# A gated mix of two attention layers on one core: key-value products in column tiles, numerators in three fixed tiles

## The chip, the core and the metric

The kernel runs on one core of one Trainium2 chip. A core has a matrix engine (TensorE: PE for its matmuls, PEld for its weight loads), a vector engine (DVE), an activation engine (ACT), a general engine (POOL) and a queue engine (SP) that issues most of the transfers. Matmuls write to PSUM, eight banks of 512 fp32 columns on 128 partitions; DVE and ACT read it from there. The metric is the device time of the whole program in microseconds, the median of several runs. Three runs of the kernel before took 323.28, 323.5 and 323.81 us.

## What is computed

Two attention layers work on the same 2048 x 640 input, 32 heads of 20, and a gate mixes them. Layer A is linear attention: two softmaxes (of a projection and of its negative) over 20 features of each head are the key and query features. Layer B is causal softmax attention in four segments of 512, with a memory between the segments.

```python
# layer A, per head
pq, pk = q @ w_phi, k @ w_phi
phi_q = concat(softmax(pq), softmax(-pq))
phi_k = concat(softmax(pk), softmax(-pk))
kv = phi_k.T @ v                      # features x 20
z = phi_k.sum(over tokens)            # features
o = (phi_q @ kv) / (phi_q @ z + 1e-6)
a = o @ wo
# layer B: per segment, softmax(q k^T) v mixed with (phi(q) @ M) / (phi(q) @ z);
# M and z grow by phi(k)^T v and phi(k) after each segment
out = g * a + (1 - g) * b             # g = sigmoid(x . gate_w)
```

Activations and weights are bf16, sums fp32. The kernel multiplies the layer-A query and key weights with `w_phi` first, so that features come from one product.

## The kernel before

The order of the instructions on each engine is written out by hand: within `tc.manual_schedule` every engine executes in the order in which the code emits. The part that the change edits runs in four stages.

- **Keys and values** (`emit_a1`, `emit_zmove`, lines 229 to 257). For each of 16 chunks of 128 tokens PE makes the key features' logits and the values, ACT takes exponentials of both signs into `Ek` and copies the values into `vA`, DVE sums each head's 20 features (L243) and takes reciprocals (L246), POOL multiplies to `EkSn` (L247). Two transfers per chunk move `EkSn` into `Z` (L255), so that a column sum over the 32 slices of `Z` becomes an elementwise sum on DVE.
- **Key-value products** (`emit_kv`, `emit_kvn`, from L404). The 640 features are five blocks `j` of 128, with two signs. For each (`j`, sign) PE accumulates over the chunks: weights are 128 columns of `EkSn`, the moving side is `vA`, 140 columns (the seven heads that the block touches), or two pieces of 80 where the block crosses head 16 (`j` = 2). DVE masks the result into `kvn` (L383). Between them DVE adds the `Z` slices, each to slice 0 (`emit_zadd`, L261): 9, then 4, then 18. The five loads of 800 KB with the weights for layer B and the two output projections stand on SP right behind the last `Z` moves (L428, L433).
- **Query features and the first denominators** (L515). `emit_pq` makes ten 128 x 1024 blocks of query logits (two halves of the tokens, five blocks); ACT takes the exponentials into `Eq`. After the fifth, PE transposes the `Z` sum (L266); DVE folds its 32 columns with 31 adds (`emit_zz`, L274) and masks the result into `kvd` (L277). After the ninth, PE makes the denominators of the first four chunks (L453), and `first_chain` turns them into the factors `cs`.
- **Numerators** (L583). For each of 16 chunks and each sign: DVE multiplies the numerator by its factor into `tt` (`emit_tt`, L489), PE makes the next half of a layer-B projection (`emit_next_half`: 36 halves for k, q and v, evicted by ACT, L553), and PE makes the numerator of the next chunk into the tile of this sign (`emit_num`, L443; two tiles, one per sign). In the first two chunks of each batch of four PE also makes denominators of the next batch in a tile of their own. POOL adds the two signs (L604), and SP transposes the sum into `oTA` (L620). One chunk in four, three activations and a POOL add (L625 to L629) make layer B's key features; two exponentials more stand in the last two chunks (L618).

Layer B (L635 on) then runs in steps of two heads' groups: PE makes logits with row tiles of 32 (L681), ACT takes exponentials (L685), POOL masks (L692), PE multiplies with v (L735), and projections and output products (`half_item`, `out_items`) fill the rest by a written plan. The first output products of the plan read `oTA` of the last chunk.

Of the kernel before, what the change touches and what calls it, by code (L numbers as in the profile page):

```python
# [15 lines left out]
def kernel(  # L16
# [15 lines left out]
    nc = tc.nc  # L32
# [196 lines left out]
    def emit_a1(sc):  # L229
# [17 lines left out]
        nc.gpsimd.tensor_tensor(  # L247
# [11 lines left out]
    def emit_zadd(ts):  # L259
        for t in ts:  # L260
            nc.vector.tensor_tensor(out=Z[:, 0, :], in0=Z[:, 0, :], in1=Z[:, t, :], op=ALU.add)  # L261
# [7 lines left out]
    def emit_zz(zt_ps):  # L269
        nc.vector.tensor_copy(out=zt, in_=zt_ps)  # L270
        ztv = zt.rearrange("p j (s a h b) -> p j s h b a", s=2, h=2, b=2)
        nc.vector.tensor_copy(out=zz, in_=ztv[:, :, :, :, 0, 0])
        for w in range(1, 32):
            nc.vector.tensor_tensor(out=zz, in0=zz, in1=ztv[:, :, :, :, w // 16, w % 16], op=ALU.add)  # L274
        nc.vector.tensor_tensor(out=zcol, in0=zz[:, :, :, 0], in1=zz[:, :, :, 1], op=ALU.add)
        for sgn in range(2):
            nc.vector.tensor_tensor(out=kvd[:, sgn, :, :, 0], in0=wmask,  # L277
                                    in1=zcol[:, :, sgn:sgn + 1].to_broadcast([P, KC, H]), op=ALU.mult)
# [79 lines left out]
    def emit_kv(j, sgn, scs):  # L358
        h0, h1 = (P * j) // DH, (P * j + P - 1) // DH + 1
        bk, off = int(j > 2), 0  # L360
        n = (h1 - h0) * DH
        b0 = h0 // 16
        if (sgn, j) not in kv_tiles:
            kv_tiles[sgn, j] = w2tile("kv_ps")
            if j < 2:
                kv_tiles[sgn, j + 3] = kv_tiles[sgn, j]
        for sc in scs:
            if h1 <= 16 or h0 >= 16:
                o = 321 * b0 + (h0 - 16 * b0) * DH
                parts = [(off, vA[:, sc].rearrange("p b n -> p (b n)")[:, o:o + n])]  # L370
            else:
                n0 = (16 - h0) * DH
                parts = [(off, vA[:, sc, 0, h0 * DH:320]),
                         (off + n0, vA[:, sc, 1, 0:n - n0])]
            for o, rhs in parts:
                nc.tensor.matmul(kv_tiles[sgn, j][:, bk, o:o + rhs.shape[-1]],
                                 lhsT=EkSn[:, sc, sgn, j * P:(j + 1) * P], rhs=rhs,
                                 start=(sc == 0 and o == off), stop=(sc == NCH - 1 and o == parts[-1][0]))

    def emit_kvn(j, sgn):  # L380
        h0, h1 = (P * j) // DH, (P * j + P - 1) // DH + 1
        g0 = TH[j][0]
        nc.vector.tensor_tensor(  # L383
            out=kvn[:, sgn, j, h0 - g0:h1 - g0, :],
            in0=kv_tiles[sgn, j][:, int(j > 2), 0:(h1 - h0) * DH].rearrange("p (h d) -> p h d", d=DH),
            in1=wmw[:, j, h0 - g0:h1 - g0, None].to_broadcast([P, h1 - h0, DH]), op=ALU.mult)
# [4 lines left out]
    def emit_pq(qb, j):  # L391
        Eq = Eq0[:, j] if qb == 0 else a3e.tile([P, 2, HB], BF16, name="Eq")
        pq = w2tile("pq")
        for half in range(2):
            for c in range(KC):
                nc.tensor.matmul(pq[:, half, :], lhsT=WqA[:, c, j * P:(j + 1) * P],  # L396
                                 rhs=xq[:, 2 * qb + half, c],
                                 start=(c == 0), stop=(c == KC - 1))
        pqf = pq.rearrange("p b n -> p (b n)")
# [4 lines left out]
    emit_zadd(range(1, 10))  # L404
    PAIRS = [(js, sgn) for js in ((0, 3), (1, 4)) for sgn in range(2)]
    for js, sgn in PAIRS:
        for j in js:
            emit_kv(j, sgn, range(14))
    for js, sgn in PAIRS:
        for j in js:  # L410
            emit_kv(j, sgn, range(14, NCH))
        for j in js:
            emit_kvn(j, sgn)
    emit_zadd(range(10, 14))
    for sgn in range(2):
        emit_kv(2, sgn, range(NCH))
        emit_kvn(2, sgn)
    emit_gate()
    emit_zadd(range(14, 32))
# [7 lines left out]
    for W, src in ((WkB, B_wk), (WqB, B_wq), (WvB, B_wv)):  # L427
        nc.sync.dma_start(out=W, in_=src.rearrange("(c p) n -> p c n", p=P))  # L428
# [5 lines left out]

    BATCH = [list(range(c, c + 4)) for c in range(0, NCH, 4)]
    NB = 4

    def emit_num(ch, sgn):
        qb, qc = divmod(ch, HB // P)
        t = nps.tile([P, 2, 512], F32, name=f"num{sgn}")  # L440
        for n, (j, bk, lo, hi) in enumerate(PIECES):
# [4 lines left out]
                             start=(n in FIRST), stop=(n in LAST))  # L446
        return t[:, :, 0:320].rearrange("p b (h e) -> p b h e", e=DH)

    def emit_den(t, ch, k):
        qb, qc = divmod(ch, HB // P)  # L450
        for sgn in range(2):
            for j in range(KC):
                nc.tensor.matmul(t[:, k, sgn].rearrange("p h e -> p (h e)"),  # L453
# [4 lines left out]
    def den_tile():  # L458
        return dps.tile([P, NB, 2, H, 2], F32, name="den")

    def emit_rr(t, n, o=0):
        rr = a3w.tile([P, NB, 2, H], F32, name="rr")
        nc.vector.reciprocal(out=rr[:, 0:n], in_=t[:, o:o + n, :, :, 1])
        return rr, emit_uu(t, rr, n, o)

    def emit_uu(t, rr, n, o):
        uu = a3w.tile([P, NB, 2, H], F32, name="uu", bufs=1)
        nc.vector.tensor_tensor(out=uu[:, 0:n], in0=t[:, o:o + n, :, :, 0], in1=rr[:, 0:n], op=ALU.mult)
        return uu

    def emit_dsum(uu, n):
# [3 lines left out]
        return dd  # L475

# [17 lines left out]
    def first_chain(dt):  # L494
        rr, uu = emit_rr(dt, NB)
# [19 lines left out]
    for qb in range(2):  # L515
        for j in range(KC):
            emit_pq(qb, j)
            if (qb, j) == (0, KC - 1):
                z_den = w2tile("z_den")
                zt_ps = emit_z(z_den[:, 0])  # L520
            if (qb, j) == (1, 0):
                emit_zz(zt_ps)
                open_stages()
            if (qb, j) == (1, 3):
                dt = z_den[:, 1].rearrange("p (k s h e) -> p k s h e", k=NB, s=2, e=2)
                for n in range(NB):
                    emit_den(dt, n, n)
    emit_gS()
    first_chain(dt)
    aps_stack.close()  # L530
    nps_stack = ExitStack()
    nps, dps, last_pps, pps = [nps_stack.enter_context(tc.tile_pool(
        name=n, bufs=b, space=bass.MemoryType.PSUM, reuse_waits="tile"))
        for n, b in (("nps", 1), ("dps", 1), ("last_pps", 1), ("pps", 2))]
    oTA = resB.tile([P, NCH + 1, KC, P], BF16, name="oTA")
    Msb = resB.tile([P, G, 4, DH + 1], F32, name="Msb")
    Mbd = resB.tile([P, G, 4, DH + 1], BF16, name="Mbd")

    def emit_half_mm(ps, part, sc, half):
        W = {"k": WkB, "q": WqB, "v": WvB}[part]  # L540
        for cc in range(KC):
            nc.tensor.matmul(ps, lhsT=xq[:, sc // 4, cc, sc % 4 * P:(sc % 4 + 1) * P],  # L542
                             rhs=W[:, cc, half * 320:(half + 1) * 320],
                             start=(cc == 0), stop=(cc == KC - 1))

# [18 lines left out]
    for vB in vBs:  # L564
        nc.gpsimd.memset(vB[:, :, :, DH:DH + 1], 1.0)
# [3 lines left out]
              for half in range(2)]  # L569

    def emit_next_half():
        if halves:
            emit_half(last_pps if len(halves) % 3 == 1 else pps, *halves.pop(0),
                      nc.scalar.copy if halves else nc.vector.tensor_copy)
# [5 lines left out]
    nums = [emit_num(0, 0)]  # L580
    emit_next_half()
    nums.append(emit_num(0, 1))
    for ch in range(NCH):  # L583
# [4 lines left out]
        for sgn in range(2):  # L588
            emit_tt(tt, sgn, nums[sgn], cs_of[ch])
            emit_next_half()  # L590
            if (ch, sgn) in ((4, 1), (9, 1), (14, 1)):
                emit_next_half()
            if ahead and k < 2 and sgn == 0:
                if k == 0:
                    dt = den_tile()
# [492 lines left out]
```

## Time and profile before

One execution was profiled. It took 323.34 us, and the span from its first to its last instruction is 321.6 us; the granted clock of TensorE is 1.00 throughout. By stage, in us (PE is a busy time, so pipelined matmuls that overlap count once):

| stage | from | to | PE | DVE | ACT | POOL |
|---|---|---|---|---|---|---|
| weights folded, first tokens | 0.0 | 10.3 | 8.6 | 4.2 | 5.3 | 8.5 |
| keys and values | 10.3 | 56.2 | 45.9 | 35.6 | 36.2 | 36.9 |
| key-value products | 56.2 | 66.7 | 10.5 | 10.2 | 1.8 | 2.8 |
| query features, first denominators | 66.7 | 89.7 | 23.0 | 19.2 | 17.6 | 4.2 |
| numerators | 89.7 | 131.6 | 41.3 | 35.5 | 24.4 | 34.3 |
| layer B and the outputs | 131.6 | 321.6 | 179.8 | 119.4 | 166.8 | 122.4 |

A row of the timeline reads: start, length of the group, engine, line, operation, what it writes and reads, shapes, how many; in brackets the idle time of the engine before it and what ended it. A long group of short instructions is one row. A row "SPq" is the time in which SP issues a transfer; the transfer lands later (2.6 us after its issue for a transpose into `oTA`, by the median).

### The profile page before, as it was taken

Reading aid. Unit: us, or ns where it says so; the run is one execution under the profiler, and the core shown is the slowest. Engines: PE = TensorE matmul, PEld = TensorE weight load, DVE = VectorE, ACT = ScalarE, POOL = GpSimd, SP = SyncE. Lnnn points to the kernel's source line nnn. Section 1 sums busy time; section 2 is a strip of 40 time slices with the busy share of each in tenths; the row PEclk is TensorE's granted clock in tenths of the full one; section 3 lists DMA queues with packets and bytes.
Section 4 is the critical chain, followed back from the end, with each engine's and each line's share of the span. In section 5 each row is a group of like instructions: output and inputs, shape, how many; then the busy total and the mean of one; then the engine's idle time right before and its main releaser. Section 6 shows DMA issues by size and latency. Waiting matters only on the chain.

```text
span 321.6 us, 9481 instructions
## 1 busy us (share of the span) xinstructions
PE 309.1 (96%) x3904; PEld 214.1 (67%) x3904; DVE 224.1 (70%) x447; ACT 252.0 (78%) x322; POOL 209.1 (65%) x308
## 2 busy tenths in 40 slices
PE   8999999999999999999999999999999999999995
PEld 7888877964577788555566566666566666655663
DVE  3477997998799797486768577676865755454463
ACT  4677888248945545999998999999998998998953
POOL 8588599302268789756657667777776676666550
PEclk9999999999999999999999999999999999999999
DMA  7947935691016796886331354462476463322132
GB/s 227 204 117 195 209 101 142 196 366 57 0 35 110 114 149 99 156 100 78 58 67 35 66 92 83 88 94 54 78 117 93 67 125 65 74 75 52 47 88 82
DMA packets 91812, 34.19 MB, mean 106 GB/s; under 512 B 79866, under 2 KB 91770, under 8 KB 91770
## 3 DMA queue, kind: packets, MB, share of 16 engines
q1 hardware_dynamic: 91194, 32.95, 50.3%
q10 hardware_dynamic: 576, 0.66, 0.7%
q8 instruction: 30, 0.49, 0.7%
q14 instruction: 12, 0.10, 0.1%
HBM read 6.42 MB, written 2.62 MB: 28 GB/s over the span
## 4 chain that ended last, share of the span: by engine, by line
PE 36%; ACT 18%; DVE 4%; POOL 3%; issue 3%; DMA 1%; ACTq 0%; DVEq 0%
ACT PT L685 17%; PE st_ps L681 8%; PE proj L813 8%; PE nda L735 6%; PE proj L869 5%; PE proj L542 4%; PE num L443 2%; DVE Eq L845 1%; ACT ek L841 1%; PE nda L748 1%; DVE td L772 1%; PE nda L743 1%; POOL oB L775 1%; DMA oTA<-oA 1%; PE st_ps L991 1%
## 5 line engine op out<-in xcount | busy, mean ns | idle before, releaser
L685 ACT ACTIVATE PT<-st_ps 128x1024 bf16<-128x1024 f32 x160 | 153.6, 1024 | 14.6 <-PE st_ps L681 12.2
L692 POOL TENSOR_SCALAR_AFFINE_SELECT PT<-PT 128x512 bf16<-128x512 bf16 (+1 forms) x130 | 85.9, 679 | 47.6 <-ACT PT L685 47.4
L735 PEld LDWEIGHTS <-PT 128*128 128x128 bf16 x1280 | 40.4, 96 | 8.8 <-issue 5.2
L247 POOL TENSOR_TENSOR EkSn<-Ek,krec 128x1280 bf16<-128x1280 bf16 x16 | 37.5, 2358 | 8.8 <-DVE krec L246 8.1
L735 PE MATMUL nda<-vB,PT 128*128 128x21 bf16 x1240 | 41.4, 173 | 0.3
L869 PEld LDWEIGHTS <-xTf 128*128 128x128 bf16 x300 | 26.5, 97 | 15.8 <-issue 6.7
L875 DVE CAST Z<-proj 128x320 bf16<-128x320 f32 x44 | 20.8, 486 | 22.0 <-PE proj L869 20.9
L235 PEld LDWEIGHTS <-xTf 128*128 128x128 bf16 x240 | 27.1, 113 | 5.8
L243 DVE TENSOR_REDUCE ksum<-Ek 128x64 f32<-128x1280 bf16 x16 | 23.6, 1475 | 7.6 <-ACT Ek L239 7.4
L681 PE MATMUL st_ps<-Z 32*128 32x512 bf16 (+3 forms) x256 | 25.0, 299 | 3.8 <-ACT PT L685 3.6
L489 DVE TENSOR_TENSOR tt<-num,rr 128x640 f32<-128x640 f32 x32 | 24.8, 802 | 4.9 <-POOL rr L482 2.2
L239 ACT ACTIVATE Ek<-pk 128x640 bf16<-128x640 f32 x32 | 20.8, 702 | 9.2 <-PE pk L235 8.2
L604 POOL TENSOR_TENSOR oA<-tt 128x640 bf16<-128x640 f32 x16 | 24.6, 1547 | 4.6 <-DVE tt L489 3.4
L813 PE MATMUL proj<-WkA,oTA 128*128 128x320 bf16 x160 | 27.1, 299 | 0.1
L681 PE MATMUL st_ps<-Eq 32*128 32x512 bf16 (+3 forms) x256 | 25.0, 299 | 2.0 <-ACT PT L685 1.6
L775 POOL TENSOR_TENSOR oB<-td 128x320 bf16<-128x320 f32 x22 | 19.5, 888 | 6.4 <-DVE td L772 4.7
L401 ACT ACTIVATE Eq<-pq 128x1024 bf16<-128x1024 f32 x20 | 19.4, 1021 | 5.4 <-PE pq L396 5.4
L813 PE MATMUL proj<-WvA,oT 128*128 128x320 bf16 x120 | 22.2, 300 | 0.6 <-DVE oTA L822 0.6
L396 PE MATMUL pq<-xTf,WqA 128*128 128x512 bf16 x100 | 22.1, 379 | 0.0
L772 DVE TENSOR_TENSOR td<-nda,rec 128x640 f32<-128x640 f32 x23 | 19.0, 824 | 2.1
L542 PEld LDWEIGHTS <-xTf 128*128 128x128 bf16 x180 | 16.3, 97 | 4.4
L443 PE MATMUL num<-kvn,Eq 128*128 128x240 bf16 (+2 forms) x192 | 18.0, 229 | 0.6 <-DVE tt L489 0.6
(174 smaller groups left out, 551.9 us busy)
## 6 DMA issues: line engine op xcount, KB each, us to landing
Z<-EkSn SPq DMA_DIRECT2D x32, 160.0 KB, 2.7
out_dram<-orow SPq DMA_DIRECT2D x8, 160.0 KB, 1.8
out_dram<-oTA SPq DMA_DIRECT2D x6, 160.0 KB, 1.9
WvA<-in_A_wqkv_dram SPq DMA_DIRECT2D x2, 400.0 KB, 6.7
WkB<-in_B_wk_dram SPq DMA_DIRECT2D x1, 800.0 KB
WqB<-in_B_wq_dram SPq DMA_DIRECT2D x1, 800.0 KB, 6.6
WvB<-in_B_wv_dram SPq DMA_DIRECT2D x1, 800.0 KB, 9.5
WkA<-in_A_wo_dram SPq DMA_DIRECT2D x1, 800.0 KB, 11.2
```

The lines of the kernel that those rows point to most:

```text
L235: nc.tensor.matmul(ps[:, bk, 0:n], lhsT=key_tokens(c, sc), rhs=rhs, start=(c == 0), stop=(c == KC - 1))
L247: nc.gpsimd.tensor_tensor(out=EkSn[:, sc].rearrange("p s (h f) -> p (s h) f", f=DH), in0=Ek.rearrange("p s (h f) -> p (s h) f", f=DH), in1 ...
L443: nc.tensor.matmul(t[:, bk, (lo - 16 * bk) * DH:(hi - 16 * bk) * DH], lhsT=Eqs[qb, j][:, sgn, qc * P:(qc + 1) * P], rhs=kvn[:, sgn, j, lo ...
L489: nc.vector.tensor_tensor(out=tt[:, sgn].rearrange("p (b h) d -> p b h d", b=2), in0=ps, in1=csb, op=ALU.mult)
L542: nc.tensor.matmul(ps, lhsT=xq[:, sc // 4, cc, sc % 4 * P:(sc % 4 + 1) * P], rhs=W[:, cc, half * 320:(half + 1) * 320], start=(cc == 0), s ...
L604: nc.gpsimd.tensor_tensor(out=oA.rearrange("p (h d) -> p h d", d=DH), in0=tt[:, 0], in1=tt[:, 1], op=ALU.add)
L681: nc.tensor.matmul(ps[:, i - i0, o:o + L - c * P], lhsT=kT[32 * i:32 * i + 32, c * P:(c + 1) * P], rhs=qT[32 * i:32 * i + 32, c * P:L], st ...
L685: nc.scalar.activation(out=PT[:, i0:i0 + 2], in_=ps, func=ACT.Exp, scale=SCALE_B)
L692: nc.gpsimd.affine_select(out=v, in_=v, pattern=[[0, n_i], [1, P]], compare_op=ALU.is_ge, fill=0.0, base=0, channel_multiplier=-1)
L735: nc.tensor.matmul(nd[:, j, i], lhsT=block(st, c)[:, i, (j - c) * P:(j - c + 1) * P], rhs=vB[:, c, 4 * st.g + i, :], start=(c == 0), stop= ...
L813: nc.tensor.matmul(ps, lhsT=oT[:, k % KC], rhs=W[:, k % KC, hs], start=(k == 0), stop=(k == n - 1))
L869: nc.tensor.matmul(ps, lhsT=xq[:, sc // 4, k, sc % 4 * P:(sc % 4 + 1) * P], rhs=W[:, k, half * 320:(half + 1) * 320], start=(k == 0), stop ...
```

## The change

Four things are edited.

1. The key-value products, but for the first chunk, are made in two column tiles: weights of 64 columns of `EkSn`, the moving side the four heads (80 columns) that these 64 features touch, written to partitions 0 to 63 or 64 to 127 of one PSUM tile that holds both signs. Blocks 0 to 3 run over chunks 1 to 13 first, then over 14 and 15; block 4 comes last. One `kvn` instruction covers both signs.
2. The `Z` adds are made in two halves of 320 columns, and `emit_zz` in slices of three and two blocks, without its first copy; `kvd` is one instruction. The last chunk's `EkSn` is made by DVE. The gate's `emit_gS` moves ahead of the last adds.
3. The layer-B and output weights wait for `kvn` of block 3 by a POOL copy into `WvB`, which is loaded first. The v projections of chunks 0 and 4 move ahead of the numerators.
4. Numerators go round three fixed tiles, made three steps ahead, and the denominators of the next batch lie in columns 320 to 447 of the numerator tiles of the batch's second chunk. All projection halves use one pool of two tiles. The key-feature activations and the two late exponentials are placed at other steps (`KEYS`, `EXPS`); the last projection half then stands in chunk 14 and the last POOL add in chunk 13, where both stood in chunk 15. Layer B's PSUM pools are laid out anew, with one pool for each logits tile.

```diff
@@ emit_a1
-        nc.gpsimd.tensor_tensor(
+        (nc.vector if sc == NCH - 1 else nc.gpsimd).tensor_tensor(
             out=EkSn[:, sc].rearrange("p s (h f) -> p (s h) f", f=DH),
...
     def emit_zadd(ts):
         for t in ts:
-            nc.vector.tensor_tensor(out=Z[:, 0, :], in0=Z[:, 0, :], in1=Z[:, t, :], op=ALU.add)
+            for lo in (0, D // 2):
+                cols = slice(lo, lo + D // 2)
+                nc.vector.tensor_tensor(out=Z[:, 0, cols], in0=Z[:, 0, cols], in1=Z[:, t, cols], op=ALU.add)
@@ emit_zz
-        nc.vector.tensor_copy(out=zz, in_=ztv[:, :, :, :, 0, 0])
         for w in range(1, 32):
-            nc.vector.tensor_tensor(out=zz, in0=zz, in1=ztv[:, :, :, :, w // 16, w % 16], op=ALU.add)
+            for js in (slice(0, 3), slice(3, KC)):
+                nc.vector.tensor_tensor(out=zz[:, js], in0=ztv[:, js, :, :, 0, 0] if w == 1 else zz[:, js],
+                                        in1=ztv[:, js, :, :, w // 16, w % 16], op=ALU.add)
...
-        for sgn in range(2):
-            nc.vector.tensor_tensor(out=kvd[:, sgn, :, :, 0], in0=wmask,
-                                    in1=zcol[:, :, sgn:sgn + 1].to_broadcast([P, KC, H]), op=ALU.mult)
+        nc.vector.tensor_tensor(out=kvd[:, :, :, :, 0], in0=wmask[:, None].to_broadcast([P, 2, KC, H]),
+                                in1=zcol.rearrange("p c s -> p s c")[:, :, :, None].to_broadcast([P, 2, KC, H]),
+                                op=ALU.mult)
@@ emit_kv
+    def emit_kv(j, sgn, scs, group=None):
+        f0, f1 = (P * j, P * j + P) if group is None else (P * j + 64 * group, P * j + 64 * group + 64)
+        h0, h1 = f0 // DH, (f1 - 1) // DH + 1
+        base = (P * j) // DH
+        if j not in kv_tiles:
+            kv_tiles[j] = w2tile("kv_ps")
+        at = {} if group is None else {"tile_position": (0, 64 * group)}
         for sc in scs:
+            parts = [(max(h0, 16 * b), min(h1, 16 * b + 16), b) for b in range(2) if h0 < 16 * b + 16 and h1 > 16 * b]
+            for n, (lo, hi, b) in enumerate(parts):
+                nc.tensor.matmul(kv_tiles[j][f0 - P * j:f1 - P * j, sgn, (lo - base) * DH:(hi - base) * DH],
+                                 lhsT=EkSn[:, sc, sgn, f0:f1],
+                                 rhs=vA[:, sc, b, (lo - 16 * b) * DH:(hi - 16 * b) * DH],
+                                 start=(sc == 0 and n == 0), stop=(sc == NCH - 1 and n == len(parts) - 1), **at)
+
+    def emit_kv_groups(j, scs):
+        for sc in scs:
+            for sgn in range(2):
+                for group in range(2):
+                    emit_kv(j, sgn, [sc], group)
...
-    emit_zadd(range(1, 10))
...
+    emit_zadd(range(1, 7))
+    for j in range(4):
+        for first in ([0], [1, 2, 3], [], [])[j]:
+            for sgn in range(2):
+                emit_kv(first, sgn, [0])
+        emit_kv_groups(j, range(1, 14))
+    for j in range(4):
+        emit_kv_groups(j, range(14, NCH))
+        emit_kvn(j)
+    emit_zadd(range(7, 9))
     for sgn in range(2):
-        emit_kv(2, sgn, range(NCH))
-        emit_kvn(2, sgn)
+        emit_kv(4, sgn, [0])
+    emit_kv_groups(4, range(1, NCH))
+    emit_kvn(4)
     emit_gate()
-    emit_zadd(range(14, 32))
+    emit_gS()
+    emit_zadd(range(9, 32))
...
-    for W, src in ((WkB, B_wk), (WqB, B_wq), (WvB, B_wv)):
+    nc.gpsimd.tensor_copy(out=WvB[:, 0, 0:2], in_=kvn[:, 0, 3, 0, 0:2])
+    for W, src in ((WvB, B_wv), (WkB, B_wk), (WqB, B_wq)):
         nc.sync.dma_start(out=W, in_=src.rearrange("(c p) n -> p c n", p=P))
@@ emit_num, den_view
-        t = nps.tile([P, 2, 512], F32, name=f"num{sgn}")
+        t = nps[(0, 2, 1)[(2 * ch + sgn) % 3]].tile([P, 2, 512], F32, name="num")
...
+    def den_view(t):
+        return t[:, :, 320:448].rearrange("p n (s h e) -> p n s h e", s=2, e=2)
...
+    pqs, vs = [(qb, j) for qb in range(2) for j in range(KC)], list(EARLY_V)
+    for what in "pppppvzppppdvp":
...
-    nps, dps, last_pps, pps = [nps_stack.enter_context(tc.tile_pool(
+    *nps, pps = [nps_stack.enter_context(tc.tile_pool(
         name=n, bufs=b, space=bass.MemoryType.PSUM, reuse_waits="tile"))
-        for n, b in (("nps", 1), ("dps", 1), ("last_pps", 1), ("pps", 2))]
+        for n, b in (("nps0", 1), ("nps1", 1), ("nps2", 1), ("pps", 2))]
...
+    KEYS, EXPS = {1: 0, 5: 1, 9: 2, 11: 3}, {(13, 0): 'k', (14, 0): 'q'}
...
+    def emit_num_at(i):
+        if i < len(order):
+            ch, sgn = order[i]
+            t = nums[ch, sgn] = emit_num(ch, sgn)
+            if ch % 4 == 1 and ch < NCH - 4:
+                for n in range(2):
+                    emit_den(den_view(t)[:, n], ch + 3 + 2 * sgn + n)
+
+    for what in "nnhhn":
...
         for sgn in range(2):
-            emit_tt(tt, sgn, nums[sgn], cs_of[ch])
-            emit_next_half()
...
+            t = nums.pop((ch, sgn))
+            emit_tt(tt, sgn, num_view(t), cs_of[ch])
...
+            if ahead and (k, sgn) in ((1, 0), (1, 1)):
+                emit_rr(rr_n, uu, den_view(t), 2 * sgn, 2)
...
+            emit_num_at(2 * ch + sgn + 3)
+            if ch - 1 in KEYS and sgn == 0:
+                nc.scalar.activation(out=ek, in_=ek, func=ACT.Exp, scale=-1.0)
...
+        if ch - 2 in KEYS:
+            nc.gpsimd.tensor_tensor(out=phik, in0=phik, in1=ek, op=ALU.add)
```

195 lines of the change are left out of this document (85 added, 110 removed).

## The prediction

> **What bounds the kernel now.** I read the page first (busy shares), then the busy time by stage, then the timeline stage by stage, then the chain of waits over the last 200 us.
>
> ```profile
> PE 309.1 (96%) x3904; PEld 214.1 (67%) x3904; DVE 224.1 (70%) x447; ACT 252.0 (78%) x322; POOL 209.1 (65%) x308
> ```
>
> ```profile
> 56.20:66.70 10.50, 10.50 (x201) 10.40 (x200) 10.16 (x22) 1.78 (x3) 2.81 (x2) 1.00 0.78 238
> 66.70:89.70 23.00, 23.00 (x152) 11.26 (x149) 19.22 (x63) 17.63 (x19) 4.16 (x6) 1.00 0.32 109
> 89.70:131.60 41.90, 41.30 (x493) 33.61 (x492) 35.47 (x51) 24.36 (x51) 34.30 (x36) 1.00 0.67 110
> ```
>
> Columns of the stage rows: stretch, its length, busy time (and instructions) of PE, PEld, DVE, ACT, POOL, granted clock, DMA share, GB/s. In the three stages that the change edits, key-value products (56.2 to 66.7), feature products with the first denominators (to 89.7) and numerators (to 131.6), PE is idle for 0.6 us in all, at granted clock 1.00. So time there can be won by shorter PE work or by those gaps; and whatever else is late becomes a new PE gap.
>
> ```profile
> 56.24 10.44 PE L376 MATMUL kv_ps<-vA,EkSn 128*128 128x140 bf16 x192
> ...
> 66.72 10.95 PE L396 MATMUL pq<-xTf,WqA 128*128 128x512 bf16 x50
> ...
> 67.69 9.43 DVE L261 TENSOR_TENSOR Z<-Z 128x640 bf16<-128x640 bf16 x18
> ...
> 77.50 0.44 PE L266 MATMUL z_den<-ident_b,Z 128*128 128x128 bf16 x5
> ...
> 78.85 6.59 DVE L274 TENSOR_TENSOR zz<-zz,zt 128x20 bf16<-128x20 bf16 x31
> ...
> 85.68 0.58 DVE L277 TENSOR_TENSOR kvd<-wmask,zcol 128x160 bf16<-128x160 f32 x2
> ...
> 86.42 1.33 PE L453 MATMUL z_den<-kvd,Eq 128*128 128x64 bf16 x40
> ```
>
> Beside PE runs a second chain that only just keeps up: DVE's Z sums end at 67.69 + 9.43 = 77.12 and PE transposes them at 77.50; DVE's `kvd` ends at 86.26 and PE uses it at 86.42. Slack: 0.4 and 0.2 us.
>
> ```profile
> 100.07 0.56 PE L443 MATMUL num<-kvn,Eq 128*128 128x240 bf16 x6 [0.30 <-DVE tt L489]
> ...
> 131.31 1.54 POOL L604 TENSOR_TENSOR oA<-tt 128x640 bf16<-128x640 f32 x1 [1.26 <-issue]
> ...
> 132.81 1.34 POOL L629 TENSOR_TENSOR Z<-Z,ek 128x640 bf16<-128x640 bf16 x1
> ...
> 132.92 2.57 SPq L620 DMA_TRANSPOSE oTA<-oA  x2
> ...
> 136.90 0.66 PEld L813 LDWEIGHTS <-oTA 128*128 128x128 bf16 x6 [0.48 <-DMA oTA<-oA]
> ```
>
> The gap at 100.07 comes again at 111.05: a numerator waits until DVE has emptied its tile. Into the last stage leads the last `oA`: ready at 132.85, its transpose second in SP's pair at 132.92, landed at about 136.87, where PE waits for it.
>
> **Key-value products.** Before: 128 matmuls of 140 columns and 64 of 80. In the trace the first start 60.8 ns apart, the second 35.8: 7.78 + 2.29 = 10.07 us (the row has 10.44, with 0.2 of last latency). After: 12 of these stay whole (first chunk; 8 x 60.8 + 4 x 35.8 ns = 0.63 us) and 300 of 64 x 80 come in 150 pairs, one per column half.
>
> No row has column tiles, so the pair is bounded. Low end: both stream at once, 35.8 ns. High end: one after the other, 71.6 ns. Nearest rows: the L681 row tiles go two at a time; with 128 columns two start within 4 ns and the next two 66 ns later (133.26), 13 ns above what 128 columns take, so 33 + 13 = 46 ns for 80. And a load with a short matmul never steps faster than in "219.76 1.00 PE nda L735 x40", 25 ns, so 50 for two. I take 48: 7.2 us. The tile shape changes six times (whole to halves and back, three times); around L681 each such change leaves some 0.09 us (L869 at 135.37 streams 0.14 us, L681 starts at 135.60): 0.55 us. Sum 7.2 + 0.63 + 0.55 = 8.4, a gain of **1.7 us** (ends: 3.5 gain, 1.85 loss; break-even for the stage is (10.07 - 1.18) / 150 = 59 ns).
>
> The Trainium skill ("TensorEngine Tiling (Array Packing)", Restrictions) says that column tiling turns Fast Weight Load off, and "TensorE: Matmul & The Clock Gate" (LDWEIGHTS) gives a plain load columns / 1.2 ns. By these, an estimate: 2 x 53 = 107 ns per pair, 16 us, a loss of 7 us in place of my gain. No run here shows it; the trace's loads are all 128 wide, 97 ns long, and at L735 25 ns apart.
>
> **The Z chain.** It must shorten too, since PE reaches the Z transposes at 77.50 - 1.7 + 1.36 (two projection halves, 2 x 0.68 us by the L542 groups, now stand ahead) = 77.2. (a) The last `EkSn` goes from POOL (2.36 us, to 59.01) to DVE: 1280 elements as in L243, 1.49 us, behind POOL's running one: about 56.65 to 58.2. The first Z add before began at 56.70 but lasted 2.66 us, until POOL was done, where the others last 0.49; so adds effectively began at 58.87 and now at 58.2. (b) Adds wait for the one before: 0.526 us apart, 31 of them 16.3 us. Halves wait for the one before last. Length of a half from 20 elements in 0.178 us (L274) and 640 in 0.492: 0.33; independent neighbours overlap by 0.084 (L383: 0.294 long, 0.210 apart): 0.246 apart, 62 of them 15.2 us. If they did not overlap it would be 22.6. (c) Five `kvn` of 280 at 0.294 + 0.146 - 0.084 = 0.36: 1.8 us, 0.5 less than ten. (d) The gate's three small operations (0.69 us) move ahead of the last adds, to which five hand-overs add 0.1. Sum: 58.2 + 15.2 + 1.8 + 0.7 + 0.1 = 76.0, 1.2 us before PE asks. From there `zz` costs as before (a pair must wait 0.17 + 0.04 us for its forerunner, 31 x 0.21), its first copy goes (0.3) and `kvd` is one instruction (0.1 less): `kvd` is ready 7.9 us after the transposes, PE asks after 40 `pq`, 8.64. Cost nothing; the cover is 0.7 us.
>
> **Weight loads held.** A POOL copy makes `WvB` wait for the fourth `kvn`, about 64.0; behind it on SP wait the other four loads, needed from 89 on, and on POOL two memsets and the stage memsets, idle there 19 us before. `WvB` must be in by 75.8; before, as third of its row it landed 9.5 us after issue, as first it will take no longer: 73.6. Nothing, with 2 us of cover; each us later would be a PE gap.
>
> **Numerators.** PE's work is the same (32 x 0.40, halves at 0.68, denominators 0.29 a chunk), only 4 halves stand earlier. With three tiles the two gaps of 0.30 us go: -0.6. DVE needs per batch of four chunks 8 x 0.745 (tt) + 2 x 0.95 + 2 x 0.29 + 0.29 + 0.94 = 9.7 us, PE 8 x 0.40 + 8 x 0.68 + 4 x 0.29 = 9.8: level, so I count a new wait of 0.1. Projection evictions share ACT with the moved exponentials (0.43 and 0.74 in 1.08 us of PE now and then); two tiles of slack hide it.
>
> **The seam.** The k and q exponentials and the last POOL add leave the end. POOL then runs cs, oA 11, add, oA 12, 13, add, 14, 15 without a pause: 1.1 + 5 x 1.53 + 2 x 1.34 after DVE's last reciprocal, so the last `oA` is no earlier against the denominators than before (46 us after their start, less the halves moved), but SP has no turn left ahead of it and lands it 2.65 us later in place of 4.0. By this side I get 0.55 us, by PE's own end 0.6 - 0.1: the same **0.55 us**.
>
> **Sum.** -1.7 - 0.55 = -2.25 us. The profiled execution took 323.34 us (span 321.6, 1.7 around it): 321.1. The median shown, 323.5, is 0.16 above that execution: **321.2**.
>
> **Rivals.** (1) *The tiles overlap fully*, 36 ns: L681's two starts within 4 ns speak for it. PE gains 3.5 us but then asks for Z at 75.4 and gets it at 76.0, so 2.9 + 0.55 count: 320.1. (2) *The tiles take turns*: L681's overlapping matmuls write two banks (line 681, `ps[:, i - i0]`), the two halves here write one. 71.6 ns: 10.74 + 1.18 = 11.9 us, +1.85 - 0.55: 324.8, slower. It decides from 63 ns per pair on. (3) *The loads set the pace*: each 64-column load takes half of the 97 ns of a 128-column row and the two go in turn, 97 ns a pair: 14.55 + 1.18 = 15.7, +5.7 - 0.55: 328.6. For it: 300 loads for 150 streams of 33 ns, nothing to hide them behind; against: 128-wide loads at 25 ns. The rule of the skill quoted above is its extreme. (4) *DVE becomes the bound*: denominators in a numerator's tile hold it until reciprocal and product are done (1.24 us more), DVE is level with PE, and the Z halves overlap less than L383. The 0.55 goes, and up to 2 us of Z wait arises: 321.8 to 323.8, middle 322.9.
>
> **Chances.** Forecast 0.46, (1) 0.20, (2) 0.12, (3) 0.09, (4) 0.13. About 0.2% (0.65 us) is what a measurement of this kernel can tell from no change. Faster: 0.46 + 0.20 + half of (4) = 0.73; within: 0.06; slower 0.21. The range reaches from full overlap with Z adds quick enough not to hold it (3.5 + 0.55: 319.4) and a further 0.7 at the seam, 318.7, to the turn-taking tiles: 325.0; it leaves out (3) and a little at both ends. The forecast's own range is 320.3 to 322.3.
>
> **What would show it.** The key-value group at 64 x 80: 300 matmuls in about 7.8 us (6 and under: rival 1; 12: 2; 15: 3). Z adds 0.25 us apart, the Z transposes with no PE idle before them. No PE wait for `tt` in the numerators beyond 0.1 us, or a new one on the denominators' tiles (4). The last transpose issued right behind its `oA`. The length of the last stage, 190 us, unchanged: if it moves by more than 0.5 us, the sum is wrong in a place where I put nothing.

## The result, and the profile after

Nine runs of each kernel on one chip: 323.43 us before (322.85 to 323.81), 322.30 us after (321.32 to 322.85); ratio 0.9964, 95% interval 0.995 to 0.9979. The forecast was 321.2. The profiled execution of the changed kernel took 322.69 us (span 321.0) where that of the kernel before took 323.34 (321.6): 0.65 us less, and 2.25 were forecast.

The page after, busy time by engine, and the stage rows (stretch, length, busy time of PE, PEld, DVE, ACT, POOL with instructions, granted clock, DMA share, GB/s):

```profile
PE 305.7 (95%) x4024; PEld 209.8 (65%) x4024; DVE 224.3 (70%) x505; ACT 253.0 (79%) x321; POOL 207.7 (65%) x308
```

```profile
56.50:65.20 8.70, 7.37 (x319) 6.66 (x319) 7.26 (x24) 1.72 (x3) 0.64 (x2) 1.00 0.41 104
65.20:91.70 26.50, 26.07 (x173) 13.13 (x170) 23.57 (x120) 18.91 (x21) 5.60 (x9) 1.00 0.45 155
91.70:129.90 38.20, 38.20 (x475) 31.70 (x474) 33.49 (x50) 23.81 (x47) 32.29 (x33) 1.00 0.74 116
```

PE has 3.4 us less to do, but in the products it is now idle for 1.3 of 8.7 us where it was never idle. The numerators have no gap any more. The timeline of the changed kernel says where PE stood (start, length, engine, line, what; in brackets idle time before it and what ended it):

```profile
56.48 6.72 PE L373 MATMUL kv_ps<-vA,EkSn 128*128 128x140 bf16 x283
...
58.34 2.90 DVE L263 TENSOR_TENSOR Z<-Z 128x320 bf16<-128x320 bf16 x12
61.71 1.56 DVE L387 TENSOR_TENSOR kvn<-kv_ps,wmw 128x280 bf16<-128x280 f32 x4 [0.47 <-PE kv_ps L373]
...
64.36 0.74 PE L373 MATMUL kv_ps<-vA,EkSn 128*64 128x80 bf16 x29 [1.16 <-issue]
...
65.14 0.45 DVE L387 TENSOR_TENSOR kvn<-kv_ps,wmw 128x280 bf16<-128x280 f32 x1 [0.93 <-PE kv_ps L373]
...
65.58 1.23 POOL L544 MEMSET vB<- 128x128 bf16 x2 [2.04 <-PE gt_ps L349]
65.64 1.21 DVE L354 TENSOR_SCALAR eg<-eg 128x16 f32<-128x16 f32 x1
...
77.99 0.58 PE L268 MATMUL z_den<-ident_b,Z 128*128 128x128 bf16 x5 [0.43 <-DVE Z L263]
...
129.82 5.22 SPq L661 DMA_TRANSPOSE oTA<-oA  x4
129.88 0.39 PE L723 MATMUL st_ps<-Z 32*128 32x512 bf16 x2
...
130.46 3.04 POOL L653 TENSOR_TENSOR oA<-tt 128x640 bf16<-128x640 f32 x2
...
136.46 0.99 PE L855 MATMUL proj<-WkA,oTA 128*128 128x320 bf16 x6 [1.02 <-DMA oTA<-oA]
```

Three waits are new, and one is larger. In the middle of block 4 PE stands still and waits for nothing that the profile shows ("issue"): 1.36 us from one start to the next. DVE, at 65.14, has stood 0.93 us for that block's `kvn`; then its small operation on `eg`, 16 numbers a partition, takes 1.21 us while POOL's two memsets run. PE waits 0.43 us for Z. And the first product with `oTA` waits 1.02 us for the last transpose.

Start to start, in the two profiled executions:

| | before | after | difference |
|---|---|---|---|
| span start to first product | 56.24 | 56.48 | +0.24 |
| first product to first `pq` | 10.48 | 8.77 | -1.71 |
| first `pq` to Z transposes, less the two early projection halves (1.36) | 10.78 | 11.38 | +0.60 |
| Z transposes to first numerator, less 1.36 again | 12.24 | 12.37 | +0.13 |
| first numerator to first `st_ps` of layer B | 41.86 | 38.16 | -3.70, of which 2.72 is the four halves moved forward: -0.98 |
| first `st_ps` to the end | 190.02 | 191.10 | +1.08 |
| sum | | | -0.64 |

So layer B begins 1.72 us earlier, and loses 1.08 of it again. The first row is start-up: over the fourteen kernels profiled here the products begin between 55.91 and 56.72.

### The profile page after: what moved, and what is told of

It reads as the page before. It is cut to its first block, busy times and chain, and to the rows that moved or that the text cites. A ratio compares the mean times of both kernels' runs of the same rounds, so it can differ in the third digit from the quotient of the medians.

```text
span 321.0 us, 9771 instructions
## 1 busy us (share of the span) xinstructions
PE 305.7 (95%) x4024; PEld 209.8 (65%) x4024; DVE 224.3 (70%) x505; ACT 253.0 (79%) x321; POOL 207.7 (65%) x308
## 4 chain that ended last, share of the span: by engine, by line
PE 62%; ACT 20%; DVE 8%; POOL 3%; DMA 3%; issue 3%; SPq 1%; ACTq 0%; DVEq 0%; POOLq 0%
ACT PT L727 17%; PE st_ps L723 8%; PE proj L855 8%; PE pk L235 7%; PE proj L531 7%; PE pv L235 6%; PE nda L777 6%; PE proj L911 5%; PE num L453 4%; PE pq L400 3%; DVE Z L263 3%; DMA x_nat<-in_A_x_dram 2%; PE kv_ps L373 2%; PE num L470 1%; DVE Eq L887 1%
## 5 line engine op out<-in xcount | busy, mean ns | idle before, releaser
L247 POOL TENSOR_TENSOR EkSn<-Ek,krec 128x1280 bf16<-128x1280 bf16 x15 | 35.1, 2360 | 9.2 <-DVE krec L246 8.5
L855 PEld LDWEIGHTS <-oTA 128*128 128x128 bf16 x160 | 13.4, 97 | 7.8 <-issue 2.7
```

The source lines that it names most:

```text
L247: (nc.vector if sc == NCH - 1 else nc.gpsimd).tensor_tensor(out=EkSn[:, sc].rearrange("p s (h f) -> p (s h) f", f=DH), in0=Ek.rearrange("p ...
L855: nc.tensor.matmul(ps, lhsT=oT[:, k % KC], rhs=W[:, k % KC, hs], start=(k == 0), stop=(k == n - 1))
```

## The experiments

The theory after this reading: (A) two column tiles run fully side by side, but so many short instructions let PE's instruction supply run dry; (B) Z comes late because its adds stand behind block 4's `kvn` and the gate, and POOL's memsets stretch the gate; (C) layer B gives back what PE waits for the last `oTA`. All runs in one table, times as medians with their ratio to runs of the kernel before on the same chip, the rest from each one's profiled execution in us. In the two columns that start with "last start", 0.14 us (0.22 behind a product of 512 columns) is the time that the earlier product itself takes; what is above it is waiting.

| kernel | time | ratio, 95% | first product to gate | last start before Z transposes to Z | first numerator to `st_ps` | last start before first `oTA` product to it | `st_ps` to end |
|---|---|---|---|---|---|---|---|
| before | 323.4 | | 10.28 | 0.22 | 41.86 | 0.45 | 190.02 |
| after | 322.30 | 0.9964 (0.995 to 0.9979) | 8.55 | 0.73 | 38.16 | 1.32 | 191.10 |
| 1 column tiles alone | 324.51 | 1.0035 (1.0022 to 1.0047) | 9.20 | 0.57 | 43.62 | 0.26 | 190.03 |
| 1b the same, idle PSUM tile | 325.40 | 1.006 (1.0039 to 1.0082) | 10.93 | 0.22 | 43.62 | 0.19 | 190.06 |
| 1c the same, other banks | 322.79 | 0.9992 (0.9976 to 1.0009) | 9.33 | 0.22 | 41.86 | 0.46 | 190.04 |
| 2 without column tiles | 324.18 | 1.0033 (1.0018 to 1.0048) | 10.23 | 0.72 | 38.16 | 0.99 | 190.75 |
| 3 two blocks whole | 323.22, one run | | 8.28 | 0.73 | 38.17 | 1.82 | 191.97 |
| 4 no hold | 323.78, one run | | 9.31 | 0.64 | 38.17 | 1.55 | 191.45 |
| 5 memset late | 321.89 | 0.995 (0.9937 to 0.9963) | 8.83 | 0.14 | 38.16 | 1.00 | 191.09 |
| 6 half a `pq` first | 324.33, one run | | 7.77 (without it) | 1.81 | 38.16 | 1.63 | 192.40 |
| 7 early `oA` | 321.73 | 0.9942 (0.9927 to 0.9956) | 8.57 | 0.73 | 38.16 | 1.61 | 191.39 |
| 8 all together | 320.72 | 0.9921 (0.9908 to 0.9935) | 7.92 (without it) | 0.14 | 38.18 | 0.91 | 190.67 |
| 9 early `oA`, turn behind | 321.45 | 0.9945 (0.9925 to 0.9965) | 8.51 | 0.72 | 38.16 | 0.14 | 190.25 |
| 10 all, turn behind | 319.47 | 0.988 (0.9865 to 0.9895) | 7.19 (without it) | 0.14 | 38.17 | 0.14 | 190.10 |

**2, the column tiles undone.** In the changed kernel every product is whole again:

```diff
-                for group in range(2):
-                    emit_kv(j, sgn, [sc], group)
+                emit_kv(j, sgn, [sc])
```

> The changed kernel with the column tiles undone: each product whole, 128x128 weights by 140 to 160 columns. Theory: one product every 63 ns, two instructions each, so no dry stretch; products to first pq 10.5 us instead of 8.77, TensorE asks for Z 1.7 us later and does not wait for it (0.43 in the changed kernel), sum +1.3: about 323.6. Rival, the changed kernel's gain comes from the numerators' ring and not from the column tiles: same time as the changed kernel, 322.3. Rival, the dry stretch belongs to the place (block 4, what runs beside it): it is there too, 1.2 to 1.4 us, and the products take 11.8 us.

The products take 10.23 us and PE is never idle in them, as the theory said. The time is 1.9 us above the changed kernel's, and 0.33% above that of the kernel before: the rest of the change alone loses, and column tiles turn it into a gain. (In three of its ten runs the granted clock was 0.993 or 0.994 and they took 325.3 to 325.4 us; the other seven took 323.4 to 324.5, by the median still 0.65 above the kernel before.) But the Z part of the expectation failed. PE comes 1.6 us later to the Z transposes and still waits as long (0.72). So the wait isn't a race between PE and a busy DVE: the adds end a fixed time behind block 4's products, whenever these end (13.0 us after the start of its `kvn` in the changed kernel, 12.9 in run 2).

**3 and 4, the idle stretch.** Run 3 makes blocks 0 and 1 whole (`for group in ((None,) if j < 2 else range(2))`) and leaves block 4 as it is; run 4 leaves out the POOL copy that holds the loads.

> The changed kernel with blocks 0 and 1 whole and blocks 2 to 4 in column tiles: block 4 is the same to the instruction. Theory, instruction supply: up to block 4 120 fewer instructions over 1.6 us more time, the supply keeps up: no idle stretch in block 4 (or under 0.4 us), products to first pq about 9.1 us, kvn of block 4 earlier, Z not waited for; 322.0 to 322.6. Rival, block 4 itself or what runs beside it stalls: 1.2 to 1.4 us idle in it again, products 10.4 us, about 323.5.

> The changed kernel without the small POOL copy that holds the five weight loads behind the key-value products; they start some 6 to 8 us earlier. Theory: the idle stretch in block 4 is instruction supply and stays, 1.2 to 1.7 us (perhaps longer, since the instruction fetch now shares the DMA engines with the loads); Z adds the same; 322.0 to 322.9. Rival, the stretch comes from the held loads starting at that moment: it goes, products to first pq 7.5 us, 321.0 to 321.5.

Run 3, timeline of PE:

```profile
56.41 8.35 PE L373 MATMUL kv_ps<-vA,EkSn 128*128 128x140 bf16 x252
64.69 0.26 PE L346 MATMUL gt_ps<-xg,back 128*128 128x12 bf16 x4
...
77.64 0.58 PE L268 MATMUL z_den<-ident_b,Z 128*128 128x128 bf16 x5 [0.43 <-DVE Z L263]
```

One unbroken group: block 4 is the same, and the idle stretch is gone, although 60 pairs were replaced by slower whole products; the stage even got 0.27 us shorter. In run 4 the stretch stays, 1.71 us, with another of 0.39 ahead of it, and the products take 9.31 us. So it belongs neither to block 4 nor to the held loads: it follows how many instructions went before in how little time. A pair is four instructions (two loads, two products) in 36 ns, a whole product two in 61. The DMA view fits: from 50 to 80 us the instruction queue made 4 fetches of 16 KB in the changed kernel and 3 before, two of them 3.5 us apart (57.73 and 61.23), the second taking 1.7 us, where most take 0.9 to 1.3. No row shows what PE's queue holds; the places where PE stops, told under run 6, show the supply as the cause. In time neither run shows a gain (single runs, and Z still waits 0.73 and 0.64). Run 3's time is 0.6 us above what was expected, with the longest distance before `oTA` of all (1.82). Run 4's is 0.9 above, and its longer idle stretch came through Z to layer B (first `st_ps` 130.62 for 129.88).

**6, long products ahead of block 4.** The first five 512-column products of the first `pq` are issued between block 3 and block 4:

```diff
     emit_zadd(range(7, 9))
+    begin_pq(0, 0, 1)
     for sgn in range(2):
         emit_kv(4, sgn, [0])
```

> The changed kernel with the first five 512-column products of the first pq (1.07 us, ten instructions) ahead of block 4. Theory, instruction supply: in that time the next fetch lands, block 4's idle stretch falls from 1.36 us to at most 0.3. But Z's chain hangs on block 4 (kvn, gate, 46 half adds) and TensorE now has 1.07 us less work behind it before it asks for Z, so the wait there grows from 0.43 to about 1.5 us and nothing is won: 321.9 to 322.7. Rival, block 4 itself causes the stretch: it stays at 1.3 us, Z is 1.1 us later, about 323.3.

Timeline of run 6, PE (one of the five long products is missing from the records):

```profile
56.53 5.77 PE L373 MATMUL kv_ps<-vA,EkSn 128*128 128x140 bf16 x250
62.40 1.24 PE L402 MATMUL pq<-xTf,WqA 128*128 128x512 bf16 x4
63.48 0.89 PE L373 MATMUL kv_ps<-vA,EkSn 128*128 128x140 bf16 x28
64.63 0.82 PE L373 MATMUL kv_ps<-vA,EkSn 128*64 128x80 bf16 x34 [0.26 <-issue]
```

The idle stretch in block 4 falls from 1.36 to 0.46 us start to start (at most 0.3 was expected), and the products without that half take 7.77 us for 8.55. As expected nothing is won, since Z hangs on block 4: PE's distance before Z grows from 0.73 to 1.81. The time is 1.6 us above the expectation; in this execution the granted clock was 0.50 from 137.2 to 140.6 us, where the changed kernel had 1.00.

These lines also show the cause of the idle stretch. In run 6 PE stops behind 250 + 28 key-value products and the five long ones, 283 in all; the changed kernel stops behind 283 as well (the row x283 above), though five more of them belong to block 4 there. In all eleven such stops (0.39 us or more, with nothing to wait for; in eight kernels) PE has made either 155 or 283 products since the first key-value product. The two places are 128 products and 128 loads apart, and over the whole changed kernel the instruction queue (q8 of its page) made 31 fetches of 16 KB for 8048 loads and products, one per 260. Each time PE goes on 1.3 to 1.5 us after a fetch has landed (62.90 and 64.36 in the changed kernel). So a stop goes with the count of instructions, not with a block, and it ends with a fetch.

**5, the memsets.** POOL's two memsets go back behind the opening of the numerators' pools:

```diff
-    for vB in vBs:
-        nc.gpsimd.memset(vB[:, :, :, DH:DH + 1], 1.0)
     def emit_zsum():
...
     nc.gpsimd.tensor_copy(out=Msb[:, :, :, DH], in_=epsm[:, None, :].to_broadcast([P, G, 4]))
+    for vB in vBs:
+        nc.gpsimd.memset(vB[:, :, :, DH:DH + 1], 1.0)
```

> The changed kernel with POOL's two memsets of vB moved back behind the opening of the numerators' pools, so that POOL stands still while VectorE works on the gate. Theory: the Z adds stand in a row behind block 4's kvn and the gate, so their end moves by what the gate takes: the operation on eg falls from 1.05 to 1.21 us to about 0.2, Z ends 0.9 us earlier, TensorE's wait of 0.43 before the Z transposes goes, numerators and everything behind start 0.4 us earlier: 321.9. Rival, the adds themselves are too slow (46 halves): wait and time stay, 322.3.

Timeline of run 5, DVE and then PE:

```profile
65.65 0.45 DVE L387 TENSOR_TENSOR kvn<-kv_ps,wmw 128x280 bf16<-128x280 f32 x1 [1.01 <-PE kv_ps L373]
66.15 0.17 DVE L354 TENSOR_SCALAR eg<-eg 128x16 f32<-128x16 f32 x1
...
66.73 10.91 DVE L263 TENSOR_TENSOR Z<-Z 128x320 bf16<-128x320 bf16 x46
...
77.91 0.44 PE L268 MATMUL z_den<-ident_b,Z 128*128 128x128 bf16 x5
```

The operation on `eg` takes 0.17 us for 1.21, the same 46 half adds follow it, and PE no longer waits. That settles (B) in the trace; the time is 0.4 us lower, as expected, but its interval overlaps that of the changed kernel.

**7 and 9, the seam.** Run 7 adds the last `oA` on DVE, puts POOL's last `phik` sum behind it, and issues the last four transposes ahead of the turn of queries of the same chunk:

```diff
-        nc.gpsimd.tensor_tensor(out=oA.rearrange("p (h d) -> p h d", d=DH),
+        (nc.vector if ch == NCH - 1 else nc.gpsimd).tensor_tensor(
...
+        if ch >= NCH - 4:
+            nc.sync.dma_start_transpose(out=oTA[:, ch], in_=oA)
         while turns_due:
...
-        nc.sync.dma_start_transpose(out=oTA[:, ch], in_=oA)
-        if ch - 2 in KEYS:
+        if ch < NCH - 4:
+            nc.sync.dma_start_transpose(out=oTA[:, ch], in_=oA)
+        if (ch - 2 in KEYS and ch < NCH - 4) or ch == NCH - 1:
```

> The changed kernel with the last oA added on VectorE, the last POOL sum of the exponentials (phik) behind it, and the transposes of the last four oA ahead of SP's turn of B's queries and keys. Theory: layer B loses 0.5 to 1 us because the last oTA lands at 136.4 and TensorE waits 1.02 us for it; now oA of chunk 15 ends near 131.6 instead of 133.50, its transpose is issued at 132.4 instead of 133.8 and lands near 135.0; the wait is under 0.3 us, and 0.6 to 1.0 us come through to the end: 321.3 to 321.7. Rival, layer B loses it through its PSUM pools' new order or the late turns of queries and keys: oTA lands earlier, time stays within 0.3 of 322.3.

Timeline of run 7 at the seam (SPq is SP's queue):

```profile
128.78 1.23 SPq L659 DMA_TRANSPOSE oTA<-oA  x1
...
130.10 1.26 SPq L589 DMA_TRANSPOSE Eq<-Z  x1
...
130.84 0.82 DVE L653 TENSOR_TENSOR oA<-tt 128x640 bf16<-128x640 f32 x1
...
131.46 3.90 SPq L659 DMA_TRANSPOSE oTA<-oA  x3
...
136.77 0.99 PE L858 MATMUL proj<-WkA,oTA 128*128 128x320 bf16 x6 [1.31 <-DMA oTA<-oA]
```

The last `oA` is ready at 131.66 in place of 133.50, and the product that needs it starts no earlier (136.77; 136.46 in the changed kernel). The edit moved the turn (the Eq<-Z line) back by a single place only, behind chunk 12; it still stands ahead of the other three. SP issues one transpose every 1.3 us without a pause, and that queue sets the landing, not POOL. The median is 0.6 us lower with an overlapping interval and a profiled execution of 322.99, so the trace gives no reason to call it a gain. Run 9 is run 7 with that turn behind the last transpose:

```diff
-        while turns_due:
+        while turns_due and not NCH - 4 <= ch < NCH - 1:
```

> The run with the early last oA, with one thing more: SP's turn of queries that stood between the transposes of the last four oA goes behind them. Theory: SP's queue sets the landing, one issue every 1.33 us; chunk 15's transpose is issued at 132.8 instead of 134.1 and lands at 135.4 instead of 136.7; TensorE's gap of 1.61 us before it falls to 0.3 or less, layer B takes 190.0 instead of 191.4 us: 321.0 to 321.4. Rival, the turn of queries is what layer B waits for next: the gap goes, the time stays at 322.0 to 322.6.

The same view of run 9:

```profile
128.38 5.20 SPq L659 DMA_TRANSPOSE oTA<-oA  x4
...
130.57 0.83 DVE L653 TENSOR_TENSOR oA<-tt 128x640 bf16<-128x640 f32 x1
...
133.67 4.03 SPq L589 DMA_TRANSPOSE Eq<-Z  x3
...
135.02 0.66 PEld L858 LDWEIGHTS <-oTA 128*128 128x128 bf16 x6 [0.15 <-DMA oTA<-oA]
```

Now PE loads `oTA` at 135.02, and the 0.15 us that the load waits cost the products nothing (0.14 from one start to the next). Layer B takes 190.25 us for 191.39 in run 7; the three turns behind cost nothing that shows. The profiled span is 319.9 us, 1.1 below the changed kernel's; the median of 321.45 (expected 321.0 to 321.4) is 0.85 below with intervals that overlap. The last two columns of the table carry (C) better than one run: over all fourteen kernels `st_ps` to end less the distance before the `oTA` product is 189.6 to 190.2 us, with the one exception of run 6 (190.8, clock 0.98). Layer B's own length changed by 0.6 us at most; what varies more is its wait for the last transpose.

**8 and 10, all together.** Runs 5, 6 and 7 (in run 10 with 9's move), and the gate's `gS` behind the Z adds, which are spread so that DVE doesn't stand:

```diff
-    emit_zadd(range(1, 7))
+    emit_zadd(range(1, 8))
...
-    emit_zadd(range(7, 9))
+    emit_zadd(range(8, 11))
+    begin_pq(0, 0, 1)
...
     emit_gate()
-    emit_gS()
-    emit_zadd(range(9, 32))
+    emit_zadd(range(11, 32))
+    emit_gS()
```

> All of it together: memsets late, half of the first pq ahead of block 4, seam as in the run before, and the gate's gS behind the Z adds with the adds spread so that VectorE never stands still (1 to 7, kvn, 8 to 10, kvn of block 4, 11 to 31). Theory: no idle stretch in the products (under 0.3), VectorE's work between 58.3 and Z is 31 x 0.474 + 5 x 0.42 = 16.8 us, Z at 75.3 to 75.6, TensorE asks at 76.0 and does not wait; numerators start 1.7 us earlier than in the changed kernel, and the seam gives 0.6 to 1.0: 319.6 to 320.2. Rival, ScalarE's exponentials become the bound of the stage (TensorE waits for Eq at the first numerators): half of it is lost, 320.7 to 321.3.

> The run with all together, with the same move in SP's queue: chunk 15's transpose issued at 130.4, landing at 133.0, before TensorE asks at 133.5. Theory: gap 0.91 falls to 0.2, 0.7 us come through: 319.8 to 320.2. Rival, the later turn of queries takes its place: 320.5 to 321.0.

Timeline of run 10, DVE's and PE's lines:

```profile
61.43 1.56 DVE L387 TENSOR_TENSOR kvn<-kv_ps,wmw 128x280 bf16<-128x280 f32 x4
...
63.00 1.51 PE L373 MATMUL kv_ps<-vA,EkSn 128*128 128x140 bf16 x62
...
64.93 9.97 DVE L263 TENSOR_TENSOR Z<-Z 128x320 bf16<-128x320 bf16 x42
74.79 0.18 DVE L354 TENSOR_SCALAR eg<-eg 128x16 f32<-128x16 f32 x1
...
75.73 0.44 PE L268 MATMUL z_den<-ident_b,Z 128*128 128x128 bf16 x5
...
132.90 1.04 PE L872 MATMUL proj<-WkA,oTA 128*128 128x320 bf16 x6
```

None of these lines has a wait left: block 4 runs through, Z is done at 74.90 and transposed at 75.73, `oTA` is there when PE asks. Run 10 takes 319.47 us, 2.8 below the changed kernel and 1.2% below the kernel before, 0.3 better than expected. Run 8, with the turn still among the transposes, stayed 0.5 above its expectation, and its distance before `oTA`, 0.91 us where run 10 has 0.14, is more than that difference; its products also stood still once, for 0.55 us start to start. Its rival (ScalarE's exponentials as the bound) didn't occur: first numerator to `st_ps` takes 38.18 us.

**1, 1b and 1c, column tiles alone.** The kernel before with the new `emit_kv`, `emit_kv_groups` and `emit_kvn` and their order, nothing else.

> The kernel before with the column-tile products alone (Z sum, weight loads, numerators as before). Theory: two column tiles run side by side, a pair every 36 ns, but TensorE's instruction supply runs dry once for about 1.3 us inside block 4, since a pair uses up four instructions in 36 ns: key-value products to first pq 8.8 us (10.5 before, 7.5 without the dry stretch). The Z sum, still in whole adds, then comes later than TensorE asks for it, about 1 us, so that only 0.3 to 0.9 us of the 1.7 come through: 322.5 to 323.1. Rival, the dry stretch comes from the other parts of the change (held loads, the POOL copy): no stretch in block 4, the products take 7.5 us, time the same because of Z.

Slower by 0.35%, and 1.4 us above the expectation. The numerators start 1.0 us earlier (88.76; 0.3 of it is start-up), and then PE stands, by the timeline of run 1:

```profile
88.76 0.56 PE L444 MATMUL num<-kvn,Eq 128*128 128x240 bf16 x6
90.95 0.84 PE L543 MATMUL proj<-WkB,xTf 128*128 128x320 bf16 x5 [1.63 <-ACT Eq L402]
```

The projection half doesn't read `Eq`; what it takes over from the last exponential is a PSUM bank. Five product tiles in place of six shift which of the four PSUM tiles each later `pq` gets, and in the built program the last one now sits in banks 6 and 7, where this half goes. My first repair, one idle tile (`pad = w2tile("pad")` with a small matmul), left the last `pq` in bank 6:

> The kernel before with the column tiles alone, and one PSUM tile taken and left idle ahead of the gate, so that the turn of the four PSUM tiles is again that of the kernel before (six tiles for the products there, five with column tiles). Theory: the 1.63 us for which TensorE waited behind the first numerators in the run without this was the last pq's PSUM tile, which the first half of layer B's projections got; now that half follows the numerators at once, the 1.0 us won at the numerators' start stays up to layer B, and 0.3 to 0.8 us of it come through: 322.6 to 323.1. Rival, column tiles alone cost what the run without the pad cost (ScalarE's exponentials are the bound of the stage): 324.1 to 324.6.

It changed nothing at that wait, and with two idle stretches in the products (0.88 and 1.69 us) it came out slower still, above both of its expectations. Run 1c reorders the pools instead:

```diff
-    nps, dps, last_pps, pps = [nps_stack.enter_context(tc.tile_pool(
+    nps, pps, dps, last_pps = [nps_stack.enter_context(tc.tile_pool(
...
-        for n, b in (("nps", 1), ("dps", 1), ("last_pps", 1), ("pps", 2))]
+        for n, b in (("nps", 1), ("pps", 2), ("dps", 1), ("last_pps", 1))]
```

> The first run again (column tiles alone in the kernel before), with the PSUM pools of the numerators' stage in another order, so that layer B's first projection half gets banks 4 and 5, which the last but one pq held, and not banks 6 and 7 of the last pq. Theory: the 1.63 us wait for Eq behind the first numerators was that bank; it goes, the stage from the first numerators to layer B takes 41.9 us as in the kernel before instead of 43.6, and what the products win at the numerators' start (1.0 us if the products take 9.4 us; nothing if the dry stretches make them 11) comes through: 322.2 to 323.4. Rival, column tiles alone make TensorE wait for ScalarE whatever the bank: 43.6 again, 324.1 to 325.

PE's timeline in run 1c:

```profile
64.30 1.67 PE L370 MATMUL kv_ps<-vA,EkSn 128*128 128x140 bf16 x62 [2.10 <-DVE kvn L384]
...
90.52 0.56 PE L444 MATMUL num<-kvn,Eq 128*128 128x240 bf16 x6
90.92 0.84 PE L543 MATMUL proj<-WkB,xTf 128*128 128x320 bf16 x5
```

The wait is gone, and the stage takes 41.86 us as before: the bank was the cause. By the median of ten runs column tiles alone are then worth nothing that can be measured. But the granted clock differs among these runs: six at 0.999 to 1.000 took 322.38 to 322.84 us, 0.7 below the kernel before by their median, and four at 0.993 to 0.995, the profiled one among them, took 324.00 to 324.25. So the change in the products alone gains some 0.7 us where the clock stays up. More is lost because the first blocks are so quick that block 4 waits 2.10 us for a PSUM tile: the first `kvn` stands on DVE behind nine whole Z adds (57.02 to 63.89).

## Why the prediction was right, and where it was wrong

The direction and the range were right, the size twice too large, and the parts compensated each other. The range, 318.7 to 325.0 us, is wide and holds slower results too, so lying in it says little; of the forecast's own range, 320.3 to 322.3, the median is the upper end.

- **Key-value products: -1.7 forecast, -1.71 measured, for the wrong reason.** The pair was put at 48 ns. In the trace a pair takes 36 ns, with its two starts 0 to some 25 ns apart: full overlap, the low bound and rival 1. Undisturbed (run 10) the products take 7.19 us to the gate, a gain of 3.1. The changed kernel gets only 1.7 of it, since PE stood still for 1.36 us; that term wasn't in the sum at all. Pairs priced 1.8 us too long (150 x 12 ns) hid it, so the match is luck. A change of tile shape costs 0.09 us, as taken.
- **Z chain: "Cost nothing; the cover is 0.7 us" failed.** The halves were sized well (46 in 10.91 us, 0.237 apart, for 0.246). What failed is step (d) and the addition itself: it let DVE work without a break from 58.2 on, while the order puts 46 half adds behind block 4's `kvn` and the gate. DVE stood 0.47 and 0.93 us for `kvn`, and the gate's small operations took 1.0 longer under POOL's memsets, which the change had moved there and which I had costed as POOL's own idle time. Z came at 78.16 for 76.0. Run 2 shows that PE's pace doesn't enter, run 5 that the memsets decide over the wait.
- **Weight loads held: nothing, and nothing showed.** The early projection halves start behind `pq` without a wait. Run 4 gave no gain from releasing the loads.
- **Numerators: -0.5 forecast, -0.98 measured.** The two waits for `tt` are gone, no wait on the denominators took their place (rival 4), and the stage took 38.16 to 38.18 us in every kernel with the ring. Of the rest I only see that two of layer B's `st_ps` products now stand ahead of the last wait for ScalarE.
- **The seam: 0.55 gain, in the sum as one with the numerators.** "SP has no turn left ahead of it and lands it 2.65 us later" is where it failed. The landing does come 2.6 us after the issue, but the issue waits in SP's queue, with a turn of queries ahead of four transposes at 1.31 us each. PE got the last `oTA` at 136.46 for 136.91, 0.45 earlier, while it had come 1.72 us earlier to layer B. The text's own test, layer B's length unchanged at 190, spoke: 191.1.
- **Rivals.** Taking turns (2) and loads that set the pace (3) are out: 300 loads of 64 columns, some 109 ns long each, overlap and hide.

## What to carry to other kernels

When a stage gets faster, follow the second engine's chain in its own order, instruction by instruction, and mark where it must stop for the first; a sum of busy times hides the stops. Where an engine stands with nothing to wait for, count its instructions up to there in several kernels: equal counts point to the supply. At a seam, look for the queue that issues without a pause, since making its inputs earlier does nothing (run 7), and reordering it does (run 9). A part that is fast alone can cost time alone (run 1: a PSUM bank), so a change of several parts is judged only with the waits of each removed.

## What the runs showed of the hardware

- Two 64-column tiles run fully side by side: 64 x 80 pairs every 36 ns. The Trainium skill ("TensorEngine Tiling (Array Packing)", Restrictions) says that column tiling turns Fast Weight Load off. The trace shows no cost of it here; the estimate of 107 ns a pair in the prediction isn't borne out.
- PE can run out of instructions: with four in 36 ns it stood for 0.4 to 1.7 us (start to start), with nothing to wait for, in eight of the eleven kernels that had all five blocks in column tiles (not in runs 1, 1c and 10), and in neither of the two that had two or all blocks whole. The stops lie 256 loads and products apart, always at the same counts, and end 1.3 to 1.5 us after a fetch of 16 KB landed.
- Two POOL memsets that overlap (1.23 us together) held a DVE operation of 0.17 us for 1.05 to 1.21 us, in all seven kernels that had them there.
- The granted clock can fall to half for 3.4 us: in the profiled executions of run 1c (0.50 from 65.5 to 68.9 us; the first five `pq` took 12.31 us for 10.95) and of run 6 (137.2 to 140.6). Ten runs, of kernels 1b, 1c, 2, 6 and 8, had a mean clock of 0.993 to 0.995; no run of the kernel before or of the changed one did. Both stretches begin up to 1.2 us after PE had stood still for over 1 us, but run 1 stood 1.9 us and kept its clock, so why it falls isn't shown.
